# Retention, routing and two FFNs on one core: token numbers, routing steps and start-up of the retention stage rewritten

## The chip, the cores and the metric

The kernel runs on one core of a Trainium2 chip. The metric is the device time of one execution in microseconds (us). A core has a matrix engine (TensorE, PE in the rows; its weight loads are PEld), VectorE (DVE), ScalarE (ACT), GpSimd (POOL) and a queue engine that only issues transfers (SyncE, SP). Each engine works through its own instructions strictly in the order in which they stand.

## The reference

Three layers on 8 x 576 = 4608 tokens of width 512, all in 32-bit floats:

```
scores = q @ k.T / 8                      # per batch (8) and head (8), 576 x 64
ret    = scores * gamma_h ** (i - j)      # lower triangle only
x      = ret @ v                          # -> (4608, 512)

xn, en = x / (|x| + 1e-6), emb / (|emb| + 1e-6)
logits = xn @ en.T / tau                  # 8 experts
e      = argmax(logits);  gate = softmax(logits)[e]
x      = gate * (relu(x @ w1[e]) @ w2[e]) # 512 -> 1024 -> 512, one expert a token

h      = x @ w_in;  g = h * cos(h)        # 512 -> 2048
out    = g @ w_out                        # -> (4608, 512)
```

## The kernel before, in words

**Stages.** Retention with routing comes first, then the experts, then the last FFN. In the experts and the last FFN each product is three matmuls on split operands (a rounded part and a remainder), written out in `mm3` (L90 to L92).

**Retention.** It runs over 36 units of 128 tokens (`seq`), 9 units to two batches, in the causal order of a running state. A unit u does: `chunk_scores` (eight score matmuls `sc` into two PSUM banks, then two masked copies `p` on DVE, L442); `chunk_inter` (products with the running state, `ot<-qk,s`, L472); `project_next` for the unit before (matmuls `xn<-rx,xt`, L510, which turn its output to tokens by features and give its logits; `lp` on DVE; two copies into a row tile `xr` on ACT, L516; a sum of squares on ACT, L518); `chunk_state` (`st`, L450, then the new state `s` on DVE, or on ACT in the first chunk of a batch, L460); `chunk_out` (`ot<-p,kv`, L486, then `xt` on DVE, L497). K and V of a unit arrive by transfers into 7 buffers; GpSimd scales V (`kv`, L421).

**Rows.** A tile of 128 tokens has a row tile `xr` of 528 columns: 512 features and 16 that hold the token's number. The pool `rows` has 13 of them. `project` writes the numbers first, by a copy on DVE (L504).

**Routing.** After the tiles of a group (9, 9, 9, 5 and 4 tiles) `route` works out argmax and counts on DVE, and one unit later `route_rest` the place of each token (`rk` on PE, `dst`, `di`), the norm (`norm_recip`) and the gate (`gt`). `emit` then scales a row tile by its gate on ACT (L583) and scatters it to its expert's rows in DRAM by an indirect transfer that GpSimd issues (L585); two emits a unit, after a pause of one unit. A row tile can be written again when its scatter has landed.

**Order.** The order on each engine comes from a scheduler that times the program by a model; `tc.issue_after(ins)` keeps what is issued inside it behind that instruction.

**After retention.** `block_h` of expert 0 begins. `count` builds the table of expert sizes, and a branch on it (L769) stands between the first half block and the rest.

Of the kernel before, what the change touches and what calls it, by code (L numbers as in the profile page):

```python
# [21 lines left out]
P = 128  # L22
# [5 lines left out]
E = 8  # L28
# [6 lines left out]
RANK_LAG = 1  # L35
# [12 lines left out]
PREP = 1  # L48
PAD = 2
# [10 lines left out]
def retention_moe_ffn(  # L60
# [5 lines left out]
    tau,  # L66
# [51 lines left out]
    warm = bank("warm")  # L118
    for _ in range(WARM):
        MM(warm[:, :P], ones_b, ones_b, start=True, stop=True)  # L120
# [7 lines left out]
    def norm_recip(T, ssq, out):  # L128

        g, r, a = T("nr_g"), T("nr_r"), T("nr_a")  # L130
        nc.vector.tensor_scalar(g, ssq, 1e-36, None, op0=ALU.max)
        nc.scalar.activation(r, g, AF.Ln)
        nc.scalar.activation(r, r, AF.Exp, scale=-0.5)
        nc.vector.tensor_tensor(a, r, r, op=ALU.mult)
        nc.vector.tensor_tensor(a, a, g, op=ALU.mult)
# [3 lines left out]
        nc.vector.tensor_scalar(r, r, 1e-6, None, op0=ALU.add)  # L139
        nc.vector.reciprocal(out, r)  # L140

# [236 lines left out]
    ecnt = const.tile([P, 1], BF16, name="ecnt")  # L378

    with ExitStack() as actx:  # L380
# [3 lines left out]
        rows = actx.enter_context(tc.tile_pool(name="rows", bufs=13))  # L384
# [5 lines left out]
        emb_s = acon.tile([E, DM], F32, name="emb_s")  # L390
        tau_s = acon.tile([P, 1], F32, name="tau_s")
# [41 lines left out]
        def chunk_scores(u, c, r):  # L433
# [6 lines left out]
            for a in range(2):  # L440
                t = tp.tile([P, NP, CH], F32, tag=f"p{a}", name=f"p{a}_{u}")
                nc.vector.tensor_tensor(t, sc[a].rearrange("p (a n) -> p a n", a=NP), tri, op=ALU.mult)  # L442
# [59 lines left out]
        def project(t, xt, lp, ssq, i):  # L502
            xr = rows.tile([P, XW], F32, tag="xr", name=f"xr_{t}")
            nc.vector.tensor_copy(xr[:, DM:], ids_s[:, t : t + 1].to_broadcast([P, XW - DM]))  # L504
            xv = xr[:, :DM].rearrange("q (m j a d) -> q a m j d", m=2, j=2, a=2)
            for a in range(2):
# [9 lines left out]
                nc.scalar.copy(xv[:, a], pv[:, :, :P].rearrange("p m (j d) -> p m j d", j=2))  # L516
            jk = small.tile([P, DM], F32, tag="junk", name=f"jk_{t}", bufs=1)
            nc.scalar.activation(jk, xr[:, :DM], AF.Square, accum_out=ssq[:, i : i + 1])  # L518
            return xr

        def route(g, t0, n, lp, ssq, xrs):
# [22 lines left out]
            cb = small.tile([P, E], BF16, tag="cb", name=f"cb_{g}")  # L544
            nc.vector.tensor_copy(cb, cnt)
            tc_ = small.tile([P, E], F32, tag="tc", name=f"tc_{g}")
            nc.vector.tensor_reduce(tc_, ohb.rearrange("p a b -> p b a"), axis=AX.X, op=ALU.add)
            nc.vector.tensor_tensor(cnt, cnt, tc_, op=ALU.add)
            return lambda: route_rest(T, g, t0, n, ec, bc, dl, ohb, cb, ssq, xrs)

        def route_rest(T, g, t0, n, ec, bc, dl, ohb, cb, ssq, xrs):
            rk = bank(f"rk_{g}")
            MM(rk[:, : n * E], tri_b, ohb.rearrange("p a b -> p (a b)"), start=True, stop=False)
            MM(rk[:, : n * E], ones_b, cb.unsqueeze(1).to_broadcast([P, n, E]), start=False, stop=n == 1)
            for k in range(1, n):
                MM(
                    rk[:, k * E : n * E],
                    ones_b,
                    ohb[:, : n - k].rearrange("p a b -> p (a b)"),
                    start=False,  # L560
                    stop=k == n - 1,
                )
            dst = T("dst", [E])
            nc.vector.tensor_tensor(dst, rk[:, : n * E].rearrange("p (a b) -> p a b", a=n), ec(1), op=ALU.add)
            nc.vector.tensor_tensor(dst, dst, ohb, op=ALU.mult)
            df = T("df", [])
            nc.vector.tensor_reduce(df, dst, axis=AX.X, op=ALU.add)
            di = T("di", [], U32)
            nc.vector.tensor_copy(di, df)
            nrm = T("nrm", [])  # L570
            norm_recip(lambda nm: T(nm, []), ssq, nrm)
            ex = T("ex", [E])
            nc.vector.tensor_tensor(ex, dl, bc(nrm), op=ALU.mult)
            early["exp"] = nc.scalar.activation(ex, ex, AF.Exp)
            gt = T("gt", [])
            nc.vector.tensor_reduce(gt, ex, axis=AX.X, op=ALU.add)
            nc.vector.tensor_scalar(gt, gt, 1e-9, None, op0=ALU.add)
            nc.vector.reciprocal(gt, gt)
            nc.vector.tensor_scalar(gt, gt, 1.0 / TWO_PI, None, op0=ALU.mult)
# [12 lines left out]

            todo.extend([lambda: None] * PAD)
            for i in range(n):
                todo.append(lambda i=i: emit(i))
            if g == EARLY:
                todo.append(lambda: early.update(rows=load_rows(0, "0_0", natp[0], HCS[0])))

        rtau = acon.tile([P, 1], F32, name="rtau")
# [3 lines left out]
        def prepare_experts():  # L603
            nc.vector.reciprocal(rtau, tau_s)
            nc.scalar.activation(small.tile([P, DM], F32, tag="junk", name="esq", bufs=1)[:E], emb_s, AF.Square, accum_out=en)
            norm_recip(lambda nm: acon.tile([E, 1], F32, name=f"e_{nm}"), en, en)
            nc.vector.tensor_scalar(emb_s, emb_s, en, rtau[:E], op0=ALU.mult, op1=ALU.mult)
            pe_ = bank("pe_")
            ep = acon.tile([E, DM], F32, name="emb_p")
# [22 lines left out]
        def project_next(xt):  # L632
# [8 lines left out]
            if i == GROUPS[g] - 1:  # L641
                cur["g"] += 1
                rest = route(g, gstart[g], GROUPS[g], cur["lp"], cur["ssq"], cur["xrs"])
                if g == EARLY:
                    nc.vector.tensor_copy(ecnt, cnt[:, 0:1])
                return rest

        for i in range(AHEAD):
# [4 lines left out]
        ranks = []  # L653
# [9 lines left out]
        for i, (b, c) in enumerate(seq):  # L663
# [7 lines left out]
            tick(2)  # L671
# [4 lines left out]
            while pend:  # L676
                rest = project_next(pend.pop(0))
                if rest is not None:
                    ranks.append([RANK_LAG, rest])
            if c < NCH - 1:  # L680
                state[(b, c)] = chunk_state(i, c, r, prev)
            xt = chunk_out(i, c, r, pr, ot)
            if i == 0:
                prepare_experts()
# [371 lines left out]
```

## Time and profile before

| | |
|---|---|
| time, median of 3 runs | 1451.93 us (1451.36 to 1456.85) |
| the profiled execution, its own time | 1452.47 us |
| its span | 1450.6 us |
| mean granted clock of TensorE | 0.985 |
| PE busy | 1411.6 us (97%) |
| DVE / ACT / POOL busy | 703.8 / 570.2 / 567.2 us |

The span runs from the first to the last profiled instruction; the 1.87 us around it belong to the time but not to the trace. Busy shares are means over stages that differ much, and a busy PE isn't one at full clock: 1.00 in a column PEclk is 2.4 GHz, 0.50 is 1.2 GHz.

### The profile page before, as it was taken

To read this page: it belongs to the slowest core of one execution; us is meant where nothing else is said; L and a number is where in the kernel's file an instruction comes from. 1 tells how busy PE (TensorE), PEld (TensorE's weight loads), DVE (VectorE), ACT (ScalarE), POOL (GpSimd) and SP (SyncE) were. 2 spreads that over 40 slices of the span, in tenths; PEclk is the share of its full clock that TensorE was granted. 3 is DMA by queue.
4 is the path that set the end of the run, shared out by engine and by line. 5 is a ranking of instruction groups with operands and counts; after the bars stand their busy time and mean duration, and the time that the engine had idled before them with its cause. 6 is when DMAs were issued, how large, how long until landed. Compare 5 with 4: busy or idle time off the path is not lost.

```text
span 1450.6 us, 23897 instructions
## 1 busy us (share of the span) xinstructions
PE 1411.6 (97%) x9321; PEld 1242.0 (86%) x9321; DVE 703.8 (49%) x1344; ACT 570.2 (39%) x1032; POOL 567.2 (39%) x401
## 2 busy tenths in 40 slices
PE   8888999999999999999999999999999999999997
PEld 6777789999999999998888888888888888888885
DVE  5666663656555666324544344444434444344432
ACT  2434453433444444334533333343333333333332
POOL 2455333655555556435532232323223232232322
PEclk8989999999999999999999999999999999999999
DMA  9878625656556656333101001010100101000000
GB/s 359 309 265 267 225 105 178 204 176 208 177 170 210 190 190 205 126 108 132 59 30 29 1 30 30 29 30 22 36 2 30 30 30 30 1 29 1 29 0 30
DMA packets 76282, 156.42 MB, mean 108 GB/s; under 512 B 6944, under 2 KB 31700, under 8 KB 76164
## 3 DMA queue, kind: packets, MB, share of 16 engines
q1 hardware_dynamic: 68946, 134.34, 28.4%
q0 software_dynamic: 5760, 19.17, 3.4%
q8 instruction: 75, 1.23, 0.4%
q10 hardware_dynamic: 1458, 1.33, 0.3%
q14 instruction: 43, 0.35, 0.1%
HBM read 117.45 MB, written 37.36 MB: 107 GB/s over the span
## 4 chain that ended last, share of the span: by engine, by line
PE 82%; issue 1%; POOL 0%; DVE 0%; ACT 0%; POOLq 0%; ACTq 0%; DVEq 0%
PE f L90 9%; PE f L92 9%; PE f L91 9%; PE o L91 9%; PE o L90 9%; PE o L92 9%; PE y L90 5%; PE h L90 5%; PE h L92 5%; PE y L91 5%; PE h L91 5%; PE y L92 5%; PE xt L278 1%; PE id L266 0%; POOL g L914 0%
## 5 line engine op out<-in xcount | busy, mean ns | idle before, releaser
L914 POOL TENSOR_TENSOR g<-kk,g 128x512 fp32r<-128x512 f32 x143 | 184.4, 1291 | 510.5 <-ACT g L913 510.3
L90 PE MATMUL f<-xf,w 128*128 128x512 f32 x576 | 224.5, 390 | 0.0
L92 PE MATMUL f<-xf,w 128*128 128x512 f32 x576 | 224.4, 390 | 0.0
L91 PE MATMUL o<-w,g 128*128 128x512 f32 x576 | 224.3, 389 | 0.0
L91 PE MATMUL f<-xf,w 128*128 128x512 f32 x576 | 224.3, 389 | 0.0
L90 PE MATMUL o<-w,g 128*128 128x512 f32 x576 | 223.9, 390 | 0.0
L92 PE MATMUL o<-w,g 128*128 128x512 f32 x576 | 219.4, 389 | 0.0
L909 ACT ACTIVATE sn<-kk 128x512 f32<-128x512 f32 x144 | 91.0, 632 | 323.5 <-DVE kk L907 323.1
L906 DVE TENSOR_SCALAR kk<-f 128x512 f32<-128x512 f32 x144 | 99.5, 691 | 240.6 <-PE f L92 234.5
L197 POOL TENSOR_TENSOR w<-st,w 128x1024 fp32r<-128x1024 f32 x68 | 164.1, 2417 | 112.7 <-ACT w L196 88.0
L911 DVE SCALAR_TENSOR_TENSOR kk<-sn,f 128x512 f32<-128x512 f32 x144 | 99.0, 688 | 183.9 <-ACT sn L910 183.7
L90 PE MATMUL y<-hs,w 128*128 128x312 f32 (+7 forms) x512 | 158.3, 310 | 0.0
L90 PE MATMUL h<-x,w 128*128 128x312 f32 (+7 forms) x512 | 155.3, 303 | 2.3 <-PEq L769 2.3
L302 ACT ACTIVATE hs<-h 128x312 fp32r<-128x312 f32 (+7 forms) x128 | 53.8, 420 | 262.6 <-PE h L92 260.8
L91 PE MATMUL h<-x,w 128*128 128x312 f32 (+7 forms) x512 | 154.4, 302 | 0.0
L92 PE MATMUL h<-x,w 128*128 128x312 f32 (+7 forms) x512 | 154.3, 301 | 0.0
L91 PE MATMUL y<-hs,w 128*128 128x312 f32 (+7 forms) x512 | 154.1, 301 | 0.0
L92 PE MATMUL y<-hs,w 128*128 128x312 f32 (+7 forms) x512 | 153.6, 300 | 0.0
L303 DVE SCALAR_TENSOR_TENSOR hs<-h,hs 128x312 fp32r<-128x312 f32 (+7 forms) x128 | 59.7, 467 | 165.3 <-ACT hs L302 164.9
L913 ACT CAST g<-kk 128x512 fp32r<-128x512 f32 x144 | 89.3, 621 | 114.5 <-DVE kk L911 113.7
L90 PEld LDWEIGHTS o<-w,g 128*128 128x128 f32 x576 | 108.1, 188 | 22.8 <-DVE kk L911 0.4
L92 PEld LDWEIGHTS f<-xf,w 128*128 128x128 f32 x576 | 108.2, 188 | 22.5
(163 smaller groups left out, 2476.8 us busy)
## 6 DMA issues: line engine op xcount, KB each, us to landing
st<-in_moe_w_dram SPq DMA_DIRECT2D x58, 512.0 KB
kv<-in_kv_dram SPq DMA_DIRECT2D x36, 512.0 KB
qk<-in_qk_dram SPq DMA_DIRECT2D x35, 512.0 KB
xs<-x2t SPq DMA_DIRECT2D x36, 256.0 KB
nat<-xs_d SPq DMA_DIRECT2D x16, 528.0 KB
sd<-in_moe_w_in_dram SPq DMA_DIRECT2D x16, 512.0 KB
wf<-ta SPq DMA_DIRECT2D x32, 256.0 KB
sd<-in_moe_w_out_dram SPq DMA_DIRECT2D x16, 512.0 KB
```

What stands on the lines that cost most here:

```text
L90: keep(MM(ps, lhs(0), rhs(0), start=first, stop=False))
L91: keep(MM(ps, lhs(0), rhs(1), start=False, stop=False))
L92: keep(MM(ps, lhs(1), rhs(0), start=False, stop=last))
L197: nc.gpsimd.tensor_tensor(wt[:, 1], st, wt[:, 0], op=ALU.subtract)
L278: nc.tensor.transpose(ps[:, d * n : (d + 1) * n], t[:n, c, d * P : (d + 1) * P], ident[:n, :n])
L302: last["act"] = nc.scalar.activation(h[:, 0], ps[:, :hc], AF.Relu)
L303: last["dve"] = nc.vector.scalar_tensor_tensor(h[:, 1], ps[:, :hc], 0.0, h[:, 0], op0=ALU.max, op1=ALU.subtract)
L906: nc.vector.tensor_scalar(kk, ps, MAGIC, MAGIC, op0=ALU.add, op1=ALU.subtract)
L909: nc.scalar.activation(sn, kk, AF.Sin, scale=math.pi)
L911: evac = nc.vector.scalar_tensor_tensor(kk, sn, 0.5, ps, op0=ALU.subtract, op1=ALU.mult)
L913: lasti[:] = evac, nc.scalar.copy(gt[:, 0], kk)
L914: (nc.vector if (t, m) == seqf[-1] else nc.gpsimd).tensor_tensor(gt[:, 1], kk, gt[:, 0], op=ALU.subtract)
```

## The change

- **Token numbers** are copied into the row tile on ACT, behind the tile's two feature copies, no longer on DVE. `rows` has 14 buffers.
- **Routing** falls into four parts: `route` itself, `counts`, `gates` and `places`, one a unit, each kept behind the masked scores `p` of its unit. Emits follow in the unit of `places`, three a unit; the scaling is kept behind the last sum of squares.
- **Steps with a constant alone** (`tensor_scalar`) in `norm_recip` and routing become `scalar_tensor_tensor` with a tensor as second operand; the cast of the places too; the casts of the counts go.
- **Start:** the temperature comes in the transfer of the expert vectors (8 rows of 513), no longer in one of its own. 40, 10 and 20 matmuls on a constant (`fill`) stand behind the scores, the state and the output of unit 0. `prepare_experts` comes behind the last.
- V is scaled two units ahead, no longer one.

```diff
-RANK_LAG = 1
-PREP = 1
-PAD = 2
+PREP = 2
+PER_UNIT = 3
+FILL = (40, 10, 20)
...
+    def fill(n, nm):
+        ps = bank(nm)
+        for _ in range(n):
+            MM(ps[:, :P], ones_b, ones_b, start=True, stop=True)
...
-        nc.vector.tensor_scalar(a, a, -0.5, 1.5, op0=ALU.mult, op1=ALU.add)
-        nc.vector.tensor_tensor(r, r, a, op=ALU.mult)
+        V(a, a, -0.5, g, op0=ALU.mult, op1=ALU.mult)
+        V(r, a, 1.5, r, op0=ALU.add, op1=ALU.mult)
...
-        rows = actx.enter_context(tc.tile_pool(name="rows", bufs=13))
+        rows = actx.enter_context(tc.tile_pool(name="rows", bufs=14))
...
-                nc.scalar.dma_start(emb_s, emb)
-                nc.scalar.dma_start(tau_s, tau.to_broadcast([P, 1]))
+                nc.scalar.dma_start(emb_t, emb)
...
-            nc.vector.tensor_copy(xr[:, DM:], ids_s[:, t : t + 1].to_broadcast([P, XW - DM]))
...
-                nc.scalar.copy(xv[:, a], pv[:, :, :P].rearrange("p m (j d) -> p m j d", j=2))
-            jk = small.tile([P, DM], F32, tag="junk", name=f"jk_{t}", bufs=1)
-            nc.scalar.activation(jk, xr[:, :DM], AF.Square, accum_out=ssq[:, i : i + 1])
+                moved = nc.scalar.copy(xv[:, a], pv[:, :, :P].rearrange("p m (j d) -> p m j d", j=2))
+            with tc.issue_after(moved.ins):
+                nc.scalar.copy(xr[:, DM:], ids_s[:, t : t + 1].to_broadcast([P, XW - DM]))
+            jk = xt.rearrange("p a b -> p (a b)")
+            state["act"] = nc.scalar.activation(jk, xr[:, :DM], AF.Square, accum_out=ssq[:, i : i + 1])
...
-            nc.vector.tensor_copy(di, df)
+                nc.vector.scalar_tensor_tensor(di, df, 0.0, df, op0=ALU.max, op1=ALU.max)
...
+            parts.append(counts)
+            parts.append(lambda: kept.extend(gates()))
+            parts.append(lambda: (places(*kept), todo.extend(emits)))
...
-                nc.scalar.mul(xr[:, :DM], xr[:, :DM], gt[:, i : i + 1])
+                with tc.issue_after(state["act"].ins):
+                    nc.scalar.mul(xr[:, :DM], xr[:, :DM], gt[:, i : i + 1])
...
-        def tick(n, lag=0):
-            while ranks and ranks[0][0] <= lag:
-                ranks.pop(0)[1]()
-            for r in ranks:
-                r[0] -= 1
+        def tick(n, k=1):
+            for _ in range(min(k, len(parts))):
+                with tc.issue_after(state["p"].ins):
+                    parts.pop(0)()
             for _ in range(min(n, len(todo))):
                 todo.pop(0)()
...
+            if i == 0:
+                fill(FILL[0], "fill0")
-            tick(2)
+            tick(PER_UNIT)
```

On DVE, from the output of unit 11 to the masked scores of unit 13, there stood before (the first number in a name is that of the unit or tile, so `xr_13` is the row tile of tile 13):

```order
L497 TENSOR_TENSOR xt_11_1049<-ot1_11_1007,gq_s_175 128x256
L504 COPY xr_13_1215<-misc_i_179 128x16
L442 TENSOR_TENSOR p0_12_1067<-sc0_12_1057,misc_i_179 128x512
L504 COPY xr_14_1284<-misc_i_179 128x16
L442 TENSOR_TENSOR p1_12_1069<-sc1_12_1058,misc_i_179 128x512
L513 COPY lp_1_909<-xn0_11_1087 128x16
L515 TENSOR_TENSOR lp_1_909<-xn1_11_1092,lp_1_909 128x16
L504 COPY xr_15_1353<-misc_i_179 128x16
L462 TENSOR_TENSOR s_12_1108<-st_12_1099,s_11_1039 128x256
L504 COPY xr_16_1426<-misc_i_179 128x16
```

In the change the end of that stretch on DVE reads:

```order
L591 TENSOR_REDUCE df_0_1129<-dst_0_1126 128x9
L519 TENSOR_TENSOR lp_1_983<-xn1_11_1154,lp_1_983 128x16
L592 SCALAR_TENSOR_TENSOR di_0_920<-df_0_1129 128x9
L467 TENSOR_TENSOR s_12_1170<-st_12_1161,s_11_1091 128x256
L502 TENSOR_TENSOR xt_12_1180<-ot0_12_1138,gq_s_177 128x256
L502 TENSOR_TENSOR xt_12_1180<-ot1_12_1139,gq_s_177 128x256
L447 TENSOR_TENSOR p0_13_1198<-sc0_13_1188,misc_i_180 128x512
```

The copies of token numbers, which stood ahead of masked scores up to nine units before their tile, are gone from DVE, and the steps of `places` stand between the masked scores of unit 12 and its state.

On ACT, from the gates of group 0 to the row tile that takes the buffer of tile 0, the change has these rows (L602 scales a row tile, L522 copies token numbers, L524 is the sum of squares):

```order
L602 ACTIVATE xr_0_398<-xr_0_398,gt_0_919 128x512
L602 ACTIVATE xr_1_463<-xr_1_463,gt_0_919 128x512
L602 ACTIVATE xr_2_528<-xr_2_528,gt_0_919 128x512
L520 COPY xr_11_1148<-xn0_11_1149 128x4x64
L520 COPY xr_11_1148<-xn1_11_1154 128x4x64
L522 COPY xr_11_1148<-misc_i_180 128x16
L524 ACTIVATE xt_11_1101,ssq_1_984<-xr_11_1148 128x512
L602 ACTIVATE xr_3_584<-xr_3_584,gt_0_919 128x512
...
L465 COPY s_13_1232<-st_13_1223 128x256
...
L520 COPY xr_14_1344<-xn0_14_1345 128x4x64
```

Before, the nine scalings (L583) stood in one row ahead of the copies of tile 10; now they stand by threes behind the tiles 10, 11 and 12, and the wait for the scatter of tile 0 lies at the first copy of tile 14.

On POOL the first scatters stand so in the change:

```order
L426 TENSOR_TENSOR kv_17_1022<-kv_17_1022,misc_i_180 128x512
L426 TENSOR_TENSOR kv_18_1106<-kv_18_1106,misc_i_180 128x512
L604 DMA xs_d_69<-xr_0_398,di_0_920 36864x528
L604 DMA xs_d_69<-xr_1_463,di_0_920 36864x528
...
L604 DMA xs_d_69<-xr_4_648,di_0_920 36864x528
L426 TENSOR_TENSOR kv_19_1185<-kv_19_1185,misc_i_180 128x512
L204 TENSOR_TENSOR w0_1506<-ste0_1379,w0_1506 128x1024
```

Before, the nine scatters of group 0 stood in one row between the scaling of V of unit 17 and that of unit 18; now one more scaling of V stands ahead of them, and V of unit 19 and a weight subtraction stand between the fifth and the sixth.

## Rows read from the trace of the kernel before

**Rows 1.** The page: span, and the chain that ended last, by engine.
```profile
span 1450.6 us, 23897 instructions
PE 82%; issue 1%; POOL 0%; DVE 0%; ACT 0%; POOLq 0%; ACTq 0%; DVEq 0%
```
**Rows 2.** First piece of that chain: start us, us, what.
```profile
231.84 0.19 issue
```
**Rows 3.** Stretches: length, busy us of five engines, granted clock, DMA share, GB/s.
```profile
11.04:21.28 10.24, 8.69 (x69) 6.88 (x66) 4.25 (x12) 0.00 (x0) 4.08 (x4) 0.50 1.03 410
72.48:79.31 6.83, 5.12 (x36) 4.16 (x37) 4.11 (x14) 1.38 (x4) 5.58 (x6) 0.50 0.71 230
99.79:106.61 6.82, 6.76 (x41) 5.41 (x42) 2.07 (x5) 2.08 (x7) 1.04 (x1) 0.50 0.47 174
123.68:130.51 6.83, 5.53 (x38) 4.57 (x39) 4.38 (x15) 1.37 (x4) 5.52 (x6) 0.50 0.85 301
174.88:178.29 3.41, 3.41 (x38) 3.08 (x36) 1.04 (x4) 1.55 (x5) 0.96 (x1) 0.50 0.41 159
22.38:60.73 38.35, 37.60 (x620) 32.22 (x616) 26.89 (x76) 15.99 (x43) 11.47 (x11) 1.00 0.95 353
60.73:112.93 52.20, 44.05 (x629) 36.99 (x627) 32.58 (x99) 22.73 (x56) 25.11 (x21) 0.87 0.78 259
112.93:159.17 46.24, 41.02 (x629) 34.72 (x627) 31.82 (x94) 18.53 (x50) 24.96 (x21) 0.93 0.83 284
159.17:190.71 31.54, 28.00 (x435) 23.90 (x433) 21.60 (x85) 18.34 (x46) 11.29 (x12) 0.95 0.34 124
232.00:1450.60 1218.60, 1208.01 (x6547) 1065.88 (x6547) 562.19 (x870) 474.50 (x798) 475.66 (x315) 1.00 0.25 80
```
**Rows 4.** PE's order of time at 48.4 us: the scores of unit 8.
```profile
48.43 0.60 PE L437 MATMUL sc<-qk 64*128 64x128 f32 x6
```
**Rows 5.** Order of time, the first 25 us; in brackets the idle time before, and its releaser.
```profile
1.08 4.00 PE L120 MATMUL warm<-ones_b 128*128 128x128 bf16 x42 [1.08 <-DVE ones_b L117]
8.66 0.17 DVE L604 RECIPROCAL rtau<-tau_s 128x1 f32<-128x1 f32 x1 [3.09 <-DMA tau_s<-in_moe_tau_dram]
9.34 0.69 PE L450 MATMUL st<-kv 128*64 128x64 f32 x16 [3.18 <-POOL kv L421]
14.16 2.08 PE L437 MATMUL sc<-qk 64*128 64x128 f32 x16
22.38 1.16 PE L437 MATMUL sc<-qk 64*128 64x128 f32 x16
```
**Rows 6.** Order of time around the first scatters, 60 to 85 us.
```profile
67.17 1.14 POOL L585 DMA_INDIRECT xs_d<-xr,di  x1 [0.96 <-DVE xt L497]
73.28 0.18 DVE L504 COPY xr<-misc_i 128x16 f32<-128x16 f32 x1 [5.98 <-DMA xs_d<-xr,di]
74.10 2.34 PE L486 MATMUL ot<-p,kv 128*64 128x128 f32 x16 [4.01 <-DVE p L442]
```
**Rows 7.** Order of time, the weight cast at 98 us.
```profile
98.48 1.04 ACT L196 CAST w<-ste 128x1024 fp32r<-128x1024 f32 x1 [3.35 <-DMA ste<-in_moe_w_dram]
99.84 1.27 PE L510 MATMUL xn<-rx,xt 128*128 128x136 f32 x4 [1.92 <-ACT xr L516]
```
**Rows 8.** Order of time: VectorE steps beside GpSimd's weight subtractions.
```profile
79.45 2.36 POOL L197 TENSOR_TENSOR w<-ste,w 128x1024 fp32r<-128x1024 f32 x1
79.69 3.16 DVE L504 COPY xr<-misc_i 128x16 f32<-128x16 f32 x1
200.09 2.08 DVE L533 TENSOR_TENSOR lg<-lp 128x32 f32<-128x32 f32 x1
```
**Rows 9.** Groups by line to 215 us: count, busy us, mean ns; idle before.
```profile
L516 ACT COPY xr<-xn 128x256 f32<-128x256 f32 x72 | 25.4, 370 | 88.8 <-DVE lp L513 85.6 <-DVE lp L515 2.0
L583 ACT ACTIVATE xr<-xr,gt 128x512 f32<-128x512 f32 x36 | 22.6, 708 | 4.4 <-DVE gt L579 4.4
L504 DVE COPY xr<-misc_i 128x16 f32<-128x16 f32 x36 | 11.8, 358 | 20.1 <-DMA xs_d<-xr,di 18.6 <-ACT jk L518 1.4
L518 ACT ACTIVATION_READ_ACCUMULATOR jk<-xr 128x1 f32 x36 | 6.8, 189 | 0.0
```

More of the change, by code (lines that the diff above doesn't have):

```diff
@@ L117, in retention_moe_ffn @@
     nc.vector.memset(ones_b, 1.0)
-    warm = bank("warm")
-    for _ in range(WARM):
-        MM(warm[:, :P], ones_b, ones_b, start=True, stop=True)
+    def fill(n, nm):
+        ps = bank(nm)
+        for _ in range(n):
+            MM(ps[:, :P], ones_b, ones_b, start=True, stop=True)
+    fill(WARM, "warm")
+    eps = const.tile([P, 2], F32, name="eps")
+    nc.vector.memset(eps[:, 0:1], 1e-6)
+    nc.vector.memset(eps[:, 1:2], TWO_PI)
     slot = const.tile([1, 4, E], F32, name="slot")
@@ L376, in split_expert @@
             wp[(e, p)] = split_piece(sts.pop((e, p)))
-    ecnt = const.tile([P, 1], BF16, name="ecnt")
     with ExitStack() as actx:
@@ L543, in route @@
             nc.vector.tensor_tensor(ohb, oh, bc(m2), op=ALU.is_equal)
[L544 to L561, printed above, removed]
-                )
[L563 to L568, printed above, removed]
-            nc.vector.tensor_copy(di, df)
[L570 to L579, printed above, removed]
@@ new lines, in route, with counts @@
+            nrm = T("nrm", [])
+            norm = norm_recip(lambda nm: T(nm, []), ssq, nrm)
+            gt, di = T("gt", []), T("di", [], U32)
+            cb = cbs[-1]
+            def counts():
+                next(norm)
+                tc_ = small.tile([P, E], F32, tag="tc", name=f"tc_{g}")
+                nc.vector.tensor_reduce(tc_, ohb.rearrange("p a b -> p b a"), axis=AX.X, op=ALU.add)
+                cbs.append(small.tile([P, E], BF16, tag=f"cb{g + 1}", name=f"cb_{g + 1}", bufs=1))
+                nc.vector.tensor_tensor(cbs[-1], cnt, tc_, op=ALU.add)
+                nc.vector.tensor_tensor(cnt, cnt, tc_, op=ALU.add)
@@ new lines, in gates @@
+            def gates():
+                rk = bank(f"rk_{g}")
+                MM(rk[:, : n * E], tri_b, ohb.rearrange("p a b -> p (a b)"), start=True, stop=False)
+                MM(rk[:, : n * E], ones_b, cb.unsqueeze(1).to_broadcast([P, n, E]), start=False, stop=n == 1)
+                for k in range(1, n):
+                    MM(
+                        rk[:, k * E : n * E],
+                        ones_b,
+                        ohb[:, : n - k].rearrange("p a b -> p (a b)"),
+                        start=False,
+                        stop=k == n - 1,
+                    )
+                next(norm)
+                ex = T("ex", [E])
+                nc.vector.tensor_tensor(ex, dl, bc(nrm), op=ALU.mult)
+                early["exp"] = nc.scalar.activation(ex, ex, AF.Exp)
+                return rk, ex
@@ L591, in emit @@
                 unordered("xs", ins)
-            todo.extend([lambda: None] * PAD)
-            for i in range(n):
-                todo.append(lambda i=i: emit(i))
+            emits = [lambda i=i: emit(i) for i in range(n)]
             if g == EARLY:
-                todo.append(lambda: early.update(rows=load_rows(0, "0_0", natp[0], HCS[0])))
-        rtau = acon.tile([P, 1], F32, name="rtau")
+                emits.append(lambda: early.update(rows=load_rows(0, "0_0", natp[0], HCS[0])))
+        rtau = acon.tile([E, 1], F32, name="rtau")
         en = acon.tile([E, 1], F32, name="en")
@@ L642, in project_next @@
                 cur["g"] += 1
[L643 to L646, printed above, removed]
+                route(g, gstart[g], GROUPS[g], cur["lp"], cur["ssq"], cur["xrs"])
+        parts = []
+        cbs = [small.tile([P, E], BF16, tag="cb0", name="cb_0", bufs=1)]
+        nc.vector.memset(cbs[0], 0.0)
         for i in range(AHEAD):
@@ L745, in retention_moe_ffn @@
         ids_of(0)
-        ranks.append([0, project_next(pend.pop(0))])
+        project_next(pend.pop(0))
         block_h(0, 1)
         tick(99, 99)
+        assert not parts and not todo
         block_h(0, 2)
```

55 lines of the change are left out of this document (34 added, 21 removed).

## The prediction

> **What bounds the kernel now.** I read the chain that ended last first. It is TensorE for 82% of the span [rows 1], and its first piece lies at 231.84 us, right behind the branch [rows 2]: before that point no unbroken chain of work sets the end. From 232 us on, PE is busy for 1208.01 of 1218.60 us at full clock [rows 3]. The change touches nothing there, so that stretch keeps its length, and whatever retention loses or gains ahead of it moves the end one for one, as long as what follows retention isn't late itself.
>
> Next I cut retention into stretches that hold the same work: from the scores of one unit to those of the unit nine further, since the units repeat by nine. From unit 2 (22.38 us [rows 5]) to 11, 11 to 20 and 20 to 29 PE took 38.35, 52.20 and 46.24 us for practically the same number of matmuls (620 to 629) [rows 3]. From unit 29 to 35 it took 31.54; the same six units in the first period, 2 to 8, took 48.43 - 22.38 = 26.05 [rows 4, 5]. The first period is nearly undisturbed (PE busy 37.60 of 38.35, clock 1.00), so it is the measure, and the losses are 13.85, 7.89 and 5.49, together 27.2 us.
>
> Two things make them up. PE is idle for 8.15, 5.22 and 3.54 us in these stretches; and in each the clock falls to 0.50 (1.2 of 2.4 GHz) for one or two pieces in which PE was busy for 5.12 + 6.76, 5.53 and 3.41 us [rows 3]. Idle time less the 0.75 of the good period, plus half of the busy time at the low clock, gives 13.3, 7.2 and 4.7 (the last without the 0.75: 5.2). That nearly closes, so I take half of such busy time as the price of the low clock.
>
> The order of time tells what the idle time waits for. DVE comes to a copy of token numbers for a row tile whose scatter is under way; it was issued at 67.17 and DVE stands still for 5.98 us, till 73.28. The masked scores are queued behind this copy, and PE waits for them for 4.01 us [rows 6]. The clock falls at 72.48. The groups by line put 18.6 us of DVE's waits on such copies [rows 9]. One stall in the second period is another: a weight cast on ACT waits 3.35 us for its transfer, the copies of a row tile stand behind it, and PE waits 1.92 us for their bank [rows 7]; the low clock from 99.79 follows. Its price is 1.92 + 6.76 / 2 = 5.3.
>
> **The start.** DVE waits 3.09 us for the temperature's transfer with the masked scores of unit 0 behind it, PE waits until 9.34 for V, and from 11.04 to 21.28 the clock is 0.50 [rows 3, 5].
>
> **The change, part by part.**
>
> *Token numbers to ACT, 14 rows.* DVE loses 36 copies (11.8 us busy) and their waits. That removes the stalls behind scatters: 13.85 - 5.3 = 8.5 in the second period, then 7.9 and 5.5, **21.9 us** in all. It takes in the two long copies, of which one took 3.16 us beside a GpSimd subtraction of 2.36 [rows 8]. On ACT no such copy stands in the trace; the nearest rows are its smallest step, 0.19, and the feature copy, 0.37 [rows 9]. At 0.2 that is 7 us in all, and at 0.37 13. ACT is busy for 18.53 of 46.24 us [rows 3], which covers either, except in the units of the next paragraph.
>
> The wait moves too: the first copy of tile 14 on ACT now waits for the scatter of tile 0, and behind it stand sums of squares, states and casts; PE waits for the banks. Times from the start of unit 12's scores: V of unit 18 takes the buffer that unit 11 leaves at 0; I allow 5 for its transfer and 1 for its scaling, so the scatter is issued at 6 and, at the 6 us of [rows 6], lands by 12. Tile 14 is copied in unit 15, after three units of 4.26 (38.35 / 9) and some 3 for scores, state and projection, at 15.8. So there is no wait, with 3.8 to spare; the fourteenth row gives one unit of that.
>
> *Parts behind masked scores.* The masks of a unit end some 2.5 us after its scores begin; `gates` and `places` put eight to ten steps of about 0.2 behind them, till 4.4, and state and output (0.4 and 0.8) then end at 5.7, where the next projection wants them at about 5.5 to 6. I take 0.3 a group here. ACT gets the gates at 3.6 and scales three rows (0.63 each, 22.6 / 36 [rows 9]) before the copies of tile 11, then three more before tile 12: 5.5 for the first three, 7.3 after tile 11, 9.2 after three more, 10.2 after tile 12 and its numbers, 10.6 after the state of unit 13. PE wants that state at 4.3 + 0.3 + 3.7 + 1.2 = 9.5 (unit 13 has no state product and is shorter). That is 1.1 late, **3.3 us** in three groups; bounds 0 (the scalings fit) and 7 (each wait is doubled).
>
> *Later gates.* The gates come one unit later than before, so the scatter of group 2 and the load of expert 0's first rows do too. Those rows are wanted behind the scores of unit 35, and I find their arrival within a microsecond of that. I take **0.7**; bounds 0 and 3.
>
> *Weight casts.* The three later pieces still stand on ACT between row tiles, and their fetches moved behind one more unit's K and V in SP's queue, as the cast did on ACT. I count the 5.3 us as staying; bounds: gone (-5.3), or 2 more.
>
> *Start.* With the temperature in the experts' transfer DVE isn't held until 8.66. The state of unit 0 still starts at 9.34. Then come 0.69 for it, 30 fills, 1.0 for the output, 0.8 for the four transposes: 11.8 plus fills. 42 warming matmuls of the same form took 4.00 us [rows 5], 0.095 each, partly before the clock rose; 30 cost 2.9 so, and half of that at best. The scores of unit 1 start at 13.3 to 14.7, and those of unit 2, one unit of 4.26 at full clock later, at 17.6 to 19.0 in place of 22.38: 3.4 to 4.8 saved, **4.1** taken; 0 if the clock falls all the same. The 40 fills behind the scores lie in PE's idle time ahead of 9.34.
>
> *Constant steps.* I count nothing for these. The row of 200.09 shows why: a TENSOR_TENSOR that has no constant at all was held for 2.08 us beside a subtraction on GpSimd [rows 8], and such steps stay in `route`, `gates` and `places`.
>
> The Trainium skill says more (SBUF — State Buffer, "SBUF: two separate sides"): a GpSimd instruction and a VectorE instruction that runs in a two-port mode, or has two SBUF inputs while GpSimd reads SBUF, exclude each other for a whole instruction. By that a `scalar_tensor_tensor` with a tensor as second operand is held as the plain step was, which speaks against this part of the change; the trace agrees for the copy and the TENSOR_TENSOR of [rows 8].
>
> Sum: 21.9 + 4.1 - 3.3 - 0.7 = 22.0. The profiled execution took 1452.47, 0.54 above the median; 1452.47 - 22.0 = 1430.5, and 1430 beside the median.
>
> **Rivals.** (a) *Steps held.* If a subtraction on GpSimd holds a step of the parts once in each of four groups, as at 200.09, each costs up to 1.9, which now stands between masks and outputs, and a fall of the clock may follow one or two of them (3.4 to 6.8 at half clock): 8 to 14 back, 1438 to 1444. For it: the steps keep two operands on chip. Against: only few of them met a GpSimd instruction so far.
>
> (b) *Everything goes.* The weight cast no longer stalls PE and no new wait shows: 22.0 + 5.3 + 4.0 = 31.3, 1421.
>
> (c) *The stall moves to ACT.* If scatters land more than 3.8 us later than I have it, ACT waits in place of DVE, with the copies that PE needs behind it. If three stalls as long as before come back, only the start is left: 1452.5 - 4.1 = 1448, no measurable change.
>
> (d) *Slower,* by the same place: ACT holds more than DVE did, states and casts too. It decides when each of three groups loses 9.8 us there (22.0 + 7.3, by three), so a first scatter that lands 13.6 us later than worked out. Twelve microseconds of that would need GpSimd held by a late V; its time would be about 1462.
>
> **How the numbers follow.** A measurement of this kernel tells about 0.5%, 7.3 us, from no change. Forecast (1425 to 1437): 0.47. (b): 0.13. (a): 0.20. (c): 0.12. (d): 0.08. The range takes in the forecast, (a) and (b) with its bounds: 1420 to 1446, which leaves (c) and (d), 0.20, out. Faster by over 0.5% (below 1444.7) are forecast, (b) and (a): 0.80; within it (c): 0.12; slower (d): 0.08.
>
> **What the profile would show.** Nine units take 39 to 41 us in all periods, but 44 to 46 in the second. No DVE instruction waits for a scatter. The clock is 1.00 from 4 to 22 us, and the scores of unit 2 start at 17.6 to 19.0. ACT's first copy of tile 14 starts without a wait for a DMA. Wrong would be: a wait of ACT for `xs_d` of several microseconds; PE waiting for the state of units 13, 22 and 31 for over 2 us; a low clock behind units 12 to 14; expert 0's first rows late.

## The result, and the profile after

The changed kernel takes 1438.55 us (median of 4 runs, 1435.16 to 1441.28), the kernel before 1453.15 beside it (1451.36 to 1456.85): a ratio of 0.9895, 95% interval 0.9865 to 0.9925. That is faster by more than 0.5%, inside the range, and 8.5 us above the predicted time; it lies 1.6 us above the 1425 to 1437 of the forecast itself, in the 1438 to 1444 of rival (a). Between the medians 14.6 us were gained, where 22.0 were forecast. The profiled execution, from which the rest is read, was the fastest of the four: 1435.16 us, 17.3 less than the profiled one of before.

From the page of the changed kernel, the span and the chain that ended last, by engine; they answer to [rows 1]:

```profile
span 1433.4 us, 24026 instructions
PE 83%; issue 1%; POOL 0%; DVE 0%; ACT 0%; POOLq 0%; ACTq 0%; DVEq 0%
```

Stretches of the changed kernel, with the columns of [rows 3]: units 2 to 11, 11 to 20, 20 to 29, 29 to 35, unit 35 to the branch, and three pieces at the low clock.

```profile
17.45:58.62 41.17, 38.24 (x618) 32.40 (x616) 26.45 (x68) 15.61 (x48) 12.54 (x13) 1.00 0.99 375
58.62:104.47 45.85, 40.07 (x628) 34.06 (x627) 28.51 (x88) 23.12 (x67) 25.33 (x22) 0.96 0.84 292
104.47:143.22 38.75, 38.45 (x628) 32.71 (x626) 28.73 (x78) 17.65 (x54) 23.65 (x20) 1.00 0.85 296
143.22:169.56 26.34, 25.97 (x434) 22.40 (x433) 21.91 (x80) 16.24 (x50) 12.09 (x13) 1.00 0.55 209
169.56:214.50 44.94, 38.48 (x312) 36.21 (x310) 22.30 (x84) 18.66 (x44) 13.35 (x11) 0.96 0.44 154
86.26:89.67 3.41, 3.41 (x34) 2.89 (x28) 0.35 (x2) 1.64 (x6) 2.98 (x2) 0.50 0.92 369
185.25:188.66 3.41, 3.41 (x16) 3.22 (x15) 2.03 (x15) 0.73 (x3) 0.44 (x1) 0.50 0.33 128
215.97:219.38 3.41, 3.41 (x15) 3.41 (x14) 0.48 (x1) 1.48 (x2) 0.00 (x0) 0.50 0.03 6
```

The last three periods fell from 52.20, 46.24 and 31.54 [rows 3] to 45.85, 38.75 and 26.34, by 19.0 us; the third and the fourth are as short as an undisturbed period. Unit 11 starts 2.1 us earlier than before (60.73 - 58.62). So 21.15 us are gained at the scores of unit 35 (190.71 - 169.56). Of these, 3.85 are lost again ahead of the branch, where the stretch takes 44.94 us and took 41.09 us before. 2.11 + 19.04 - 3.85 = 17.30, the whole difference. The stretch of before, from the scores of unit 35 to the gap of PE at the branch:

```profile
190.71:231.80 41.09, 36.87 (x310) 34.73 (x308) 19.94 (x79) 16.66 (x37) 12.85 (x11) 1.00 0.47 167
```

Three longer waits are left ahead of the branch. The first is in the start, here in the order of time:

```profile
4.55 0.09 DVE L621 RECIPROCAL rtau<-emb_t 8x1 f32<-8x1 f32 x1
17.45 1.16 PE L442 MATMUL sc<-qk 64*128 64x128 f32 x16
22.16 0.76 DVE L502 TENSOR_TENSOR xt<-ot,gq_s 128x256 f32<-128x256 f32 x2 [2.22 <-DMA gq_s<-c_gq_dram]
22.73 1.17 PE L514 MATMUL xn<-rx,xt 128*128 128x136 f32 x8 [2.08 <-DVE xt L502]
24.44 0.83 PE L442 MATMUL sc<-qk 64*128 64x128 f32 x10
```

The scores of unit 2 start 4.93 us earlier than before [rows 5], but the output of that unit is scaled by query factors (`gq_s` of chunk 2) that haven't landed. PE waits 2.08 us, and at unit 3 only 2.24 of the 4.93 are left (26.68 before, 24.44 now).

The second, at the weight casts, answers to [rows 7]:

```profile
76.66 2.36 POOL L204 TENSOR_TENSOR w<-ste,w 128x1024 fp32r<-128x1024 f32 x1
79.06 0.39 SPq L191 DMA_DIRECT2D ste<-in_moe_w_dram  x1
84.47 1.04 ACT L203 CAST w<-ste 128x1024 fp32r<-128x1024 f32 x1 [8.29 <-DMA ste<-in_moe_w_dram]
85.84 0.76 PE L477 MATMUL ot<-qk,s 64*64 64x128 f32 x12 [4.30 <-ACT xr L520]
```

The fourth piece's transfer needs a staging buffer, which GpSimd's first subtraction frees at 79.02; it is issued at 79.06 and its cast starts at 84.47. The cast stands ahead of a row tile's copies on ACT, and PE waits 4.30 us for their banks. The low clock of 86.26 follows, and a later cast costs PE 1.44 us more at 99.58.

The third, in the last route, answers to the row of 200.09 in [rows 8]:

```profile
178.58 4.69 POOL L204 TENSOR_TENSOR w<-st,w 128x1024 fp32r<-128x1024 f32 x2
178.73 4.60 DVE L539 TENSOR_TENSOR lg<-lp 128x32 f32<-128x32 f32 x1
184.51 0.19 PE L565 MATMUL rk<-ohb,tri_b 128*128 128x32 bf16 x1 [4.30 <-DVE ohb L549]
```

Two subtractions now stand behind each other when the last group's first step comes; it is held for 4.60 us (2.08 before), and PE waits 4.30. The low clock of 185.25 follows.

No VectorE instruction waits for a scatter any more, and the list of ACT's waits has none for one either. From 4.34 to 86.26 us the clock is 1.00. So the profile shows what the prediction wanted to see, to within 0.3 us (the periods of 41.17 and 38.75 us lie just outside 39 to 41, unit 2 starts 0.15 us earlier), and none of its signs of being wrong. The loss in the last route is a place for which it named no sign.

### The profile page after: what moved, and what is told of

Read it like the earlier page. It is cut to its first block, busy times and chain, and to the rows that moved or that the text cites. A ratio compares the mean times of both kernels' runs of the same rounds, so it can differ in the third digit from the quotient of the medians.

```text
span 1433.4 us, 24026 instructions
## 1 busy us (share of the span) xinstructions
PE 1404.9 (98%) x9392; PEld 1237.5 (86%) x9392; DVE 697.9 (49%) x1297; ACT 570.2 (40%) x1068; POOL 567.6 (40%) x401
## 4 chain that ended last, share of the span: by engine, by line
PE 83%; issue 1%; POOL 0%; DVE 0%; ACT 0%; POOLq 0%; ACTq 0%; DVEq 0%
PE f L89 9%; PE f L91 9%; PE f L90 9%; PE o L89 9%; PE o L91 9%; PE o L90 9%; PE y L89 5%; PE h L89 5%; PE h L90 5%; PE y L90 5%; PE h L91 5%; PE y L91 5%; PE xt L285 1%; PE id L273 0%; POOL g L931 0%
```

## The experiments

**The parts of the change, each alone or undone.** Token numbers on ACT, put into the kernel before:

```diff
-            nc.vector.tensor_copy(xr[:, DM:], ids_s[:, t : t + 1].to_broadcast([P, XW - DM]))
...
+            with tc.issue_after(moved.ins):
+                nc.scalar.copy(xr[:, DM:], ids_s[:, t : t + 1].to_broadcast([P, XW - DM]))
...
-        rows = actx.enter_context(tc.tile_pool(name="rows", bufs=13))
+        rows = actx.enter_context(tc.tile_pool(name="rows", bufs=14))
```

> The kernel before, with the token numbers copied on ACT behind the tile's feature copies and 14 row buffers, nothing else of the change (the sum of squares writes into xt so that 14 buffers fit). Theory: the scatter waits on VectorE were the loss, so this part alone gives most of the gain: the three stalled periods fall from 52.2, 46.2 and 31.5 us to about 45, 39 and 27, together 17 to 22 us less, ratio 0.985 to 0.988; the start stays as it was, unit 2 at 22.4 us. Rival: the gain needs the route in four parts, since nine scalings in a row now stand on ACT ahead of the row tiles: at most 10 us less, ratio above 0.993.

It took 1441.33 us (4 runs; before 1452.03), ratio 0.9914 (0.9886 to 0.9942). Unit 35 starts 13.05 us earlier; 11.0 of them are left at the end of the profiled execution, since the clock is low in its last route (191.31 to 194.72). Its stretches from unit 11 to 20, 20 to 29 and 29 to 35, columns as in [rows 3]:

```profile
60.47:110.19 49.72, 41.22 (x628) 34.59 (x627) 28.20 (x87) 22.16 (x63) 25.08 (x21) 0.93 0.79 271
110.19:149.96 39.77, 38.46 (x628) 32.69 (x626) 29.84 (x84) 19.46 (x59) 24.92 (x21) 1.00 0.92 325
149.96:177.66 27.70, 26.30 (x435) 22.51 (x433) 22.78 (x86) 18.62 (x53) 11.18 (x13) 1.00 0.41 147
```

The scatter stalls are gone without a route in parts: 39.77 and 27.70 us. In the period from unit 11 to 20 the gain was eaten at the weight casts, where PE waits 2.48, 0.77 and 4.34 us; the last of the three in the order of time:

```profile
96.43 1.04 ACT L196 CAST w<-ste 128x1024 fp32r<-128x1024 f32 x1 [4.37 <-DMA ste<-in_moe_w_dram]
97.80 1.28 PE L509 MATMUL xn<-rx,xt 128*128 128x136 f32 x4 [4.34 <-ACT xr L515]
```

So both numbers miss: 10.7 us less, where the theory had at least 17 and the rival at most 10, and by a third mechanism. The reverse, token numbers back on VectorE in the changed kernel:

```diff
+            nc.vector.tensor_copy(xr[:, DM:], ids_s[:, t : t + 1].to_broadcast([P, XW - DM]))
...
-            with tc.issue_after(moved.ins):
-                nc.scalar.copy(xr[:, DM:], ids_s[:, t : t + 1].to_broadcast([P, XW - DM]))
```

> The changed kernel with the token numbers copied on VectorE again, as in the kernel before; 14 rows, parts and start stay. Theory: VectorE waits for scatters again in each group but the first, 15 to 22 us more than the changed kernel, so 1450 to 1458 us. Rival: the route in four parts took the stall away by itself: within 5 us of the changed kernel, 1435 to 1441 us.

It took 1456.48 us (10 runs), 17.9 more than the changed kernel and 1.0025 of the kernel before (1.0011 to 1.0039). In the order of time VectorE stands still for 7.01 us behind a scatter, then the copy itself takes 3.62 beside GpSimd:

```profile
75.23 3.62 DVE L509 COPY xr<-misc_i 128x16 f32<-128x16 f32 x1 [7.01 <-DMA xs_d<-xr,di]
79.59 1.76 PE L491 MATMUL ot<-p,kv 128*64 128x128 f32 x14 [9.00 <-DVE p L447]
```

The same comes once more a group later, where PE waits 8.88 us; in the group after that it waits 0.88. The stretches, as above:

```profile
58.72:113.53 54.81, 42.33 (x629) 35.98 (x627) 33.80 (x97) 22.75 (x55) 25.58 (x22) 0.88 0.72 253
113.53:162.49 48.96, 40.08 (x628) 34.48 (x626) 31.93 (x94) 18.53 (x50) 22.98 (x19) 0.90 0.71 252
162.49:189.49 27.00, 26.12 (x435) 22.47 (x433) 21.30 (x78) 15.16 (x40) 11.83 (x12) 1.00 0.43 162
```

The theory's number holds, and without this part nothing of the gain is left. But the loss lies in the first two of these periods, which are longer than in the kernel before, and not in the last: 27.00 us, against 26.34 in the changed kernel and 31.54 before. There the rest of the change does without this part what this part does without the rest (27.70).

The start alone, in the kernel before:

```diff
-                nc.scalar.dma_start(emb_s, emb)
-                nc.scalar.dma_start(tau_s, tau.to_broadcast([P, 1]))
+                nc.scalar.dma_start(emb_t, emb)
...
+            if i == 0:
+                fill(FILL[0], "fill0")
```

> The kernel before, with the start part alone: the temperature in the experts' transfer and the 40, 10 and 20 filling matmuls. Theory: the scores of unit 2 start at 17.3 to 19 us in place of 22.4 and all later periods keep their length: 3.5 to 5 us less, ratio about 0.997. Rival: a faster start only brings forward the waits for transfers, so that by unit 11 nothing is left: ratio 1.000 and unit 11 at 60.7 us as before.

1453.7 us (10 runs), ratio 1.0006 (0.9994 to 1.0019). Unit 2 starts at 17.70 us, unit 3 at 25.34, since the factors of chunk 2 come no earlier; unit 11 starts at 59.59 (60.73 before), unit 35 at 188.93 (190.71). The wait for the factors in the order of time, and the low clock that follows it, as a stretch:

```profile
22.35 0.76 DVE L499 TENSOR_TENSOR xt<-ot,gq_s 128x256 f32<-128x256 f32 x2 [2.17 <-DMA gq_s<-c_gq_dram]
22.92 1.43 PE L512 MATMUL xn<-rx,xt 128*128 128x136 f32 x8 [2.02 <-DVE xt L499]
```

```profile
23.67:27.08 3.41, 3.41 (x36) 3.04 (x34) 1.42 (x5) 1.47 (x4) 1.04 (x1) 0.50 1.04 399
```

The rival is nearly right: of 4.7 us at unit 2, 1.1 are left at unit 11, and the runs can't tell them from nothing. The changed kernel without the fills, FILL = (0, 0, 0):

> The changed kernel without the 40, 10 and 20 filling matmuls; the temperature still comes with the experts. Theory: the fills keep the clock up; without them a low clock of several microseconds returns ahead of unit 2, whose scores start at 20.5 to 22.5 us in place of 17.45: 3 to 5 us more than the changed kernel. Rival: the start was gained by the earlier temperature alone: unit 2 at 17.5 to 18.5 us, at most 1 us more.

1441.12 us (4 runs, 1436.85 to 1441.78), not told from the changed kernel's 1438.55. Here the theory fell, and the rival's number too. The order of time, and two stretches with their clock:

```profile
14.97 1.16 PE L442 MATMUL sc<-qk 64*128 64x128 f32 x16
22.21 0.76 DVE L502 TENSOR_TENSOR xt<-ot,gq_s 128x256 f32<-128x256 f32 x2 [4.75 <-DMA gq_s<-c_gq_dram]
22.78 2.15 PE L514 MATMUL xn<-rx,xt 128*128 128x136 f32 x8 [4.61 <-DVE xt L502]
```

```profile
3.81:20.87 17.06, 11.98 (x191) 9.83 (x188) 7.93 (x26) 3.00 (x10) 5.21 (x5) 1.00 1.02 396
20.87:27.70 6.83, 4.92 (x40) 4.58 (x40) 2.19 (x7) 1.50 (x5) 2.09 (x2) 0.50 1.03 403
```

The clock is 1.00 up to 20.87 us without a fill, and unit 2 starts 2.5 us earlier than with them. PE then waits 4.61 us for the output of unit 2, which waits for the same factors; they land at 22.2 us in any case. The clock falls in that wait, and unit 11 starts at 61.17 us, with the fills at 58.62: by then the earlier start has turned into a loss in this execution.

**Three repairs in the changed kernel.** The factors issued earlier:

```diff
             raw[i] = load_chunk(i)
-            if i < 2:
-                load_consts(i)
+            load_consts(i)
...
-                load_consts(i + 2)
```

> The changed kernel with the query factors of all five chunks issued on SP behind the K and V of their own unit (units 1 to 5), no longer behind those of units 6 to 8. Theory: the output of unit 2 waits for its factors alone; the 2.08 us gap of PE ahead of tile 2's projection goes and the scores of unit 3 start at 21.7 us in place of 24.44, unit 11 at 56 us. Rival: K and V of the next units, which now arrive later, take the place of the wait: unit 3 at 23.5 us or later.

Unit 3 starts at 21.57, as the theory had it, but unit 11 at 60.66, not 56: with the factors there, the next wait comes at unit 5, where two weight casts stand ahead of a state on ACT. The one time is 1439.36. From its order of time:

```profile
31.65 1.04 ACT L203 CAST w<-ste 128x1024 fp32r<-128x1024 f32 x1 [5.83 <-DMA ste<-in_moe_w_dram]
35.06 1.01 PE L477 MATMUL ot<-qk,s 64*64 64x128 f32 x16 [4.32 <-ACT s L465]
```

The weight casts kept in their unit on ACT:

```diff
-                with tc.issue_after(state["pool"].ins):
+                with tc.issue_after(state["pool"].ins), tc.issue_after(state["act"].ins):
                     wp[(0, key)] = split_piece(st)
```

> The changed kernel with the six weight casts of the retention stage kept on ACT behind the sum of squares of the unit in which the program has them. Theory: the casts stood too early on ACT and waited for transfers that themselves wait for a staging buffer; with the order of the program no cast waits for over 1 us, the gaps of PE of 4.30 and 1.44 us in units 16 to 19 and the low clock behind them go, and the nine units from 11 to 20 take 38.5 to 40.5 us in place of 45.85. Rival: the staging buffers come free later, the transfers too, and the wait only moves to units 26 to 29: units 20 to 29 take 42 us or more.

Its stretches from unit 11 to 20, 20 to 29 and 29 to 35:

```profile
57.38:96.44 39.06, 38.27 (x628) 32.65 (x626) 30.00 (x87) 20.30 (x61) 20.20 (x19) 1.00 0.87 311
96.44:139.35 42.91, 38.67 (x628) 32.73 (x626) 34.53 (x85) 22.12 (x63) 25.13 (x21) 1.00 0.87 314
139.35:168.86 29.51, 26.03 (x434) 22.40 (x432) 24.95 (x76) 17.72 (x50) 15.48 (x13) 1.00 0.46 169
```

The 38.5 to 40.5 us of the theory came (39.06, 6.8 less), and the rival's 42 us or more in the next period too, though not by its mechanism: none of the six casts waits for a transfer. VectorE is busy for 34.53 us there, 5.8 more than in the changed kernel. So what the first period gained the next two lost again (4.2 and 3.2 us): from unit 11 to 35 the three take 111.48 us, in the changed kernel 110.94. One run, 1434.25 us. The last two pieces split behind the last scatter:

```diff
-            wp[(0, n)] = load_piece(*expert_src(0, n))
+        late = {n: fetch_piece(*expert_src(0, n), f"l{n}") for n in (6, 7)}
...
+        with tc.issue_after(state["emit"].ins):
+            for n in (6, 7):
+                wp[(0, n)] = split_piece(late[n])
```

> The changed kernel with expert 0's last two weight pieces split behind the last scatter in place of ahead of the last group's. Theory: the two GpSimd subtractions held the first step of the last route on VectorE for 4.60 us; without them it takes 0.2 us, the PE gap of 4.30 us ahead of its ranks falls to below 1.5 us and the stretch from the scores of unit 35 to the branch is 2.5 to 5 us shorter. Rival: the ranks wait for the last tile's projection and norm anyway: the gap stays above 3 us.

The first step takes 0.19 us and PE's gap ahead of the ranks is gone, as is the low clock behind it; from unit 35 to the gap at the branch it takes 36.91 us (175.22 to 212.13), in the changed kernel 42.94 (169.56 to 212.50). So 6.0 us hung there, more than the 5 expected. The one time, 1435.27, says little: its period from unit 11 to 20 took 50.93 us, with casts that are the same as in the changed kernel. All three, and no fills:

> The changed kernel with all three of these (factors early, casts kept, last pieces late) and without the 40, 10 and 20 filling matmuls. Theory: the losses add up: unit 3 at 19.5 to 20.5 us in place of 24.44 (2.7 for the factors, 2.5 for the fills, which only delayed units 1 and 2), 5 to 7 us less between units 11 and 20, 2.5 to 5 at the end, together 12 to 17 us less than the changed kernel, 1421 to 1427 us, ratio to the kernel before 0.979 to 0.983. Rival: each repair brings the next wait forward, as an earlier start did on the kernel before: at most 5 us less than the changed kernel, ratio above 0.986.

1424.11 us (4 runs, 1422.13 to 1424.97), ratio 0.9797 (0.9780 to 0.9813), 14.4 less than the changed kernel: the theory's number. Its sum came out partly by luck. The period from unit 11 to 20 is 6.9 us shorter (38.96), but the two behind it are 6.5 longer (42.44 and 29.17), which the theory didn't count; the gain of the profiled execution lies ahead of unit 11 (3.9 us), behind unit 35 (5.6 to the branch) and in the low clock behind the branch, which is gone. And unit 3 starts at 21.63, not at 20: PE waits 2.30 us for V at 6.79, and the clock is 0.50 from 8.94 to 12.35. Of the four later executions without fills, which follow below, the clock fell there in one (unit 3 at 20.85) and stayed up in three (unit 3 at 19.1 to 19.4). With fills it fell there in none of the six executions that were profiled, but unit 2 started at 17.3 to 17.9 us in them, without fills at 14.6 to 17.3. The price of the fills for the whole is not settled.

**What the parts cost when GpSimd is at work.** The order of time of the kernel with the three repairs shows what made the later periods long once the casts were kept in their units:

```profile
101.41 0.67 PE L477 MATMUL ot<-qk,s 64*64 64x128 f32 x16 [1.85 <-ACT ex L578]
102.98 2.36 POOL L204 TENSOR_TENSOR w<-ste,w 128x1024 fp32r<-128x1024 f32 x1 [3.00 <-ACT w L203]
103.03 0.22 DVE L582 TENSOR_REDUCE gt<-ex 128x9 f32<-128x72 f32 x1
103.17 0.23 DVE L588 TENSOR_TENSOR dst<-rk,misc_i 128x72 f32<-128x72 f32 x1
103.31 2.05 DVE L583 SCALAR_TENSOR_TENSOR gt<-gt,eps 128x9 f32<-128x9 f32 x1
106.73 0.96 PE L514 MATMUL xn<-rx,xt 128*128 128x136 f32 x6 [0.95 <-DVE xt L502]
```

L583, whose median is 0.16 us, is held for 2.05, till the subtraction ends, and PE waits 0.95 us for what is queued behind it; the 1.85 us before come from two such steps, beside the subtraction ahead (2.29 us) and the scaling of V behind that (0.97). The next four kernels start from this one. The casts moved to units without a part of a route:

```diff
-PIECE_AT = ((3, 2), (3, 4), (4, 0), (5, 2), (5, 4), (6, 0))
+PIECE_AT = ((3, 0), (3, 1), (3, 2), (5, 0), (5, 1), (5, 2))
```

> The kernel with the three repairs and without fills, and with the six weight casts moved to units 15, 16, 17, 24, 25 and 26, where no part of a route stands; they stood in units 17, 19, 20, 26, 28 and 29. Theory: the casts' subtractions on GpSimd held routing steps on VectorE for 0.5 to 2.3 us each in units 19 to 21 and 28 to 30, and PE's gaps of 0.8 to 1.9 us there come from that; the stretches from unit 11 to 20, 20 to 29 and 29 to 35 fall from 38.96, 42.44 and 29.17 to about 38.5, 39 and 26.5, 5 to 7 us less, 1417 to 1420 us. Rival: the gaps come from the parts themselves behind the masks, whatever GpSimd does: the three stretches stay within 1.5 us.

The same three stretches:

```profile
54.36:93.50 39.14, 38.29 (x628) 32.66 (x626) 30.10 (x87) 22.17 (x63) 24.79 (x21) 1.00 0.90 326
93.50:131.41 37.91, 37.88 (x629) 32.59 (x627) 28.24 (x88) 23.24 (x66) 22.65 (x21) 1.00 0.93 335
131.41:157.33 25.92, 25.89 (x434) 22.37 (x432) 21.28 (x73) 14.61 (x45) 14.16 (x14) 1.00 0.53 204
```

1416.44 us (4 runs, 1415.66 to 1418.97), ratio 0.9745 (0.9727 to 0.9763). The theory holds, in the last two stretches (4.5 and 3.3 us less), and the rival fell. From unit 20 to 35 PE is busy for all but 0.06 us. This version beats both kernels, by 37.4 and 22.1 us between medians.

Parts not pinned behind the masked scores (the line `with tc.issue_after(state["p"].ins):` taken out):

> The kernel with the three repairs and without fills, with the routing parts no longer kept behind the masked scores of their unit, so that they stand up to a unit earlier on VectorE. Theory: the pinning gives little, since the parts cost VectorE the same wherever they stand; within 3 us of the kernel that has it. Rival: steps that wait for ACT's logarithm and exponent then stand ahead of masked scores and outputs, which PE waits for: 1 to 2 us in each of three groups, 3 to 6 us more.

1420.36 us (4 runs), 3.75 less than with the pins; from unit 11 to 35 it takes 107.77 us in place of 110.57, and it comes to unit 11 2.1 us earlier, where the trace with the pins had the low clock in the start. The pins bring nothing here; the steps meet other subtractions without them. The rival fell. By the stretch the theory's 3 us hold, by the whole time they are just passed, and the sign wasn't expected.

Constant steps in the old form:

```diff
-                nc.vector.scalar_tensor_tensor(
-                    gt, gt, 1e-9, eps[:, 1:2].to_broadcast([P, n]), op0=ALU.add, op1=ALU.mult
-                )
+                nc.vector.tensor_scalar(gt, gt, 1e-9, TWO_PI, op0=ALU.add, op1=ALU.mult)
```

> The kernel with the three repairs and without fills, with the steps that have a constant as in the kernel before (TENSOR_SCALAR and a cast) in place of SCALAR_TENSOR_TENSOR with a second tensor. Theory: both forms are held alike beside a GpSimd subtraction, steps of either form reach 0.9 to 2.3 us there, and the stretch from unit 11 to 35 stays within 2 us of 110.57. Rival: the constant form is held longer or oftener: 4 us more or beyond.

From its order of time, the step that was held for 2.05 us:

```profile
100.83 2.36 POOL L204 TENSOR_TENSOR w<-ste,w 128x1024 fp32r<-128x1024 f32 x1 [2.84 <-ACT w L203]
101.33 1.90 DVE L583 TENSOR_SCALAR gt<-gt 128x9 f32<-128x9 f32 x1
```

The same step is held in this form as in the other; units 11 to 35 take 112.16 us, 1.6 more. One run, 1423.25. The theory holds, as far as one execution tells.

Thirteen row buffers:

> The kernel with the three repairs and without fills, with 13 row buffers in place of 14. Theory: the wait for scatters has little to spare on ACT; the first scatter is issued at 65.65 us and the copy of tile 13 stands at 70.96, so with one buffer less ACT waits 0.5 to 2 us there and again in the next groups, 1 to 5 us more between units 11 and 35. Rival: the margin of a unit that was worked out ahead is real and thirteen buffers do as well: no wait of ACT for a scatter, within 1 us.

From ACT's waits, 50 to 215 us (us in all, times, the longest):

```profile
ACT xr L520 <- DMA xs_d<-xr,di: 1.1, 2, 0.8
```

ACT waits twice for a scatter, 0.31 us at 68.95 and 0.83 at 112.16, so without the fourteenth buffer the margin is used up, as the theory had it. But behind neither wait does PE stand still. From unit 11 to 35 it is 111.88 us, 1.3 more, and that lies in the last six units (30.32 against 29.17 us), where PE waits for a routing step and the clock falls behind it:

```profile
141.93 1.13 PE L477 MATMUL ot<-qk,s 64*64 64x128 f32 x16 [2.18 <-ACT ex L578]
```

So that the buffer is worth 1 us is not shown; in this one execution (1423.73 us) its lack cost TensorE nothing that the trace shows.

## Why the prediction came out as it did

| term | predicted | measured in the profiled execution |
|---|---|---|
| scatter stalls, less scalings late | -21.9 + 3.3 | -19.04 in three periods |
| start | -4.1 | -4.93 at unit 2, -2.11 at unit 11 |
| first rows late | +0.7 | +0.16 (PE waits at 170.88) |
| last route held | 0 | +3.69 |
| sum | -22.0 | -17.30 |

This is the account of the fastest of four executions. The medians are 14.6 us apart, and the 2.7 us between the two have no trace of their own; that they lie at the weight casts (below) is likely, but not shown.

*Scatters: right in the mechanism.* Undoing this part costs 17.9 us, close to the 18.6 net, and alone it gives 10.7 of the 14.6. That the 17.9 come so close is partly luck: the prediction put 5.5 us on the copies of the last period, which stays short without this part (27.00), and the other two became longer than they had been. Two further pieces were off and nearly cancelled. ACT's scalings were not late: PE has no gap above 0.15 us in the changed kernel in units 8 to 15 nor in units 20 to 27, and none above 0.34 in units 29 to 34, where 1.1 us a group was counted. And the weight casts, counted at 5.3 with up to 2 more, took the upper bound: the period from 11 to 20 is 7.1 us longer than the next. That wait isn't steady. With the casts left as they were, this period took 45.85 us in the changed kernel, 48.22 without fills, 48.49 with early factors and 50.93 with the last pieces late, so that 44 to 46 came true is luck of this execution.

*Start: the place right, the end wrong.* Unit 2 starts at 17.45, just below the 17.6 to 19.0 worked out. The step that failed is in the sum: the 4.1 us saved at unit 2 went into it as saved at the end. (That what is gained ahead of the branch moves the end one for one held: 17.3 us there, 17.3 in the whole.) I looked for no transfer that the earlier unit would run into, and the factors of chunk 2 land at 22.2 us whatever comes first. So 4.93 us became 2.24 at unit 3 and 2.11 at unit 11; with the start alone, 1.1 of 4.7 us were left there. The prediction credited the fills with the clock. That is not shown: without them it was 1.00 from 3.81 to 20.87 us in one execution, it fell at 8 to 9 us in two of the six that were profiled, and with fills so early in none of six.

*The last route: rival (a), at one place.* I cited the row of 200.09 [rows 8] and counted nothing for it in the sum. It is the same step that was held for 4.60 us in place of 2.08, since both subtractions now stand behind each other there: PE's gap is 4.30 in place of 2.18, and half of 3.41 us at the low clock comes on top, 3.8 together. Moving the subtractions took 6.0 us away, the old part too. The rival expected a held step in each of four groups and up to 1.9 us for each; in the others the steps that met a subtraction or a scaling of V were held 0.4 to 1.8 us, and PE waited 0.34 us at most.

*Rivals (b), (c) and (d)* didn't come: the cast stall stayed, and ACT has no wait for a scatter. The margin of 3.8 us behind (c) was nearly right. In the kernel with the three repairs and no fills, where no cast stands ahead of it, the scores of unit 12 start at 59.46 us, the first scatter is issued at 65.65 and lands at 71.29, and tile 14 is copied at 74.54: 6.2, 11.8 and 15.1 us from the start of the unit, where 6, 12 and 15.8 were worked out, and 3.3 to spare. With thirteen buffers one unit of 4.26 us goes off the 3.8, which leaves a wait of 0.5, and ACT waited 0.31 and 0.83.

Two slips of the prediction don't move its forecast: the idle time and the low clock of the last period give 4.5, not 4.7 us; and (a) counts the low clock in full at its upper end, by the prediction's own price of a half it ends at 11 us, 1441.

*Constant steps: right.* Both forms are held beside GpSimd (2.05 and 1.90 us at the same step). The Trainium skill (SBUF — State Buffer, "SBUF: two separate sides") has it so for an instruction with two SBUF inputs against a GpSimd instruction that reads SBUF; the trace agrees for the new form (2.05).

Left open: the price of the fills, and what the parts of the route give by themselves, since the one run that separates them (token numbers alone) differs from the changed kernel mostly in the unsteady cast period. Which of the other parts shortens the last period, and what scaling V two units ahead does, was not run alone.

## What to carry to other kernels

Before a gain at the start is carried to the end, follow the units behind it to the next thing that comes at a fixed time: here a transfer queued behind later units' data turned 4.9 us into 2.1. Give instructions that wait for a transfer a place in each engine's order, not in the program alone: casts that stood too early on ACT made one period 6.8 us longer. But look at the periods behind before you book such a gain: kept in their units, the casts met the steps of the routing, and all of it was lost again. The 7.6 us between units 11 and 35 came only when the long GpSimd instructions were kept out of the units in which VectorE has small steps on the path.

## What the runs showed of the hardware

A VectorE step isn't held beside GpSimd as such; its kind and where its operands lie decide. In the kernel with the three repairs, during one subtraction from 102.98 to 105.34 us, a reduction over one SBUF tensor took 0.22 us, a TENSOR_TENSOR with one operand in PSUM (`dst<-rk,misc_i`) 0.23, and the next step, with two SBUF operands, 2.05, to the end of the subtraction. The masks, outputs, states and logits of this kernel, which read PSUM, are never held: in the changed kernel none of the 72 masks takes over 0.70 us, none of the 72 outputs and 24 states over 0.43 and none of the 72 steps on logits `lp` over 0.18, with or without GpSimd beside them. Of the steps that read SBUF alone, those with two operands were held, and with one operand a constant step (1.90 us) and a copy (3.62 us, with the token numbers back on VectorE), but not the reduction (0.22 us).
